# Asking the gate and up weights one section earlier: their two DMAs moved ahead of keys, rows of maxima and value rows in the sync engine's queue

## The chip, the core and the metric

The kernel runs on one core of one Trainium2 chip. The metric is the time of one execution on the device in microseconds (us). A core has five engines that run their own instruction streams: PE (TensorE, matrix products; PEld is its load of stationary data), DVE (VectorE), ACT (ScalarE), POOL (GpSimd) and SP (SyncE), which here issues all DMAs of the main part, one after the other in the order of its queue: an entry that must wait holds up all that stand behind it.

## The reference

```python
x = A_x                                   # 1 x 2048 x 576, float32
xn = _layernorm(x)
s = attention(xn, A_wqkv, A_wo)           # 32 heads of 18 columns, softmax over 2048 keys
g = silu((gelu(xn @ w_gate) * (xn @ w_up)) @ w_down)     # 576 -> 4608 -> 576
return x + s * g
```

## The kernel before

Every float32 operand of a product is cut into a high and a low part (`hi` and `lo`), and three of the four products of parts are summed. The cutting of weights is POOL's work: `split_gu` (lines 156 to 163, its two instructions at lines 131 and 133) cuts one third of a section's gate and up weights into a tile `wh` and a tile `wl`.

**Sections.** The feed-forward part is worked off in 144 sections. The tokens come in 4 blocks of 512; for each block there are 18 rounds of 2 sections, and a section makes 128 of the 4608 hidden columns for 512 tokens: 54 matmuls into `pg` and `pu` (line 548, gate in the upper and up in the lower 64 rows of the array, in pairs that run side by side). Attention is interleaved with it. Sections 0 to 9 are the lead: their extra work is the maxima of the first scores (`pm`, line 1024, reduced by DVE at line 1027). Sections 10 to 137 carry attention: 8 slots each, with scores (`pe`, line 1077, then the exponential on ACT) and the maxima of a later unit. After each odd section come the products with the values (`acc`, line 1112); so an even and an odd section make a pair that repeats. Down products (`py`) follow after a round: in rounds of the lead half of them after each section, in the rounds called PREP (sections 10 to 45, most of the first block and the start of the second) 96 half-height matmuls after each even section (line 616), from section 46 on a seven-product scheme (line 686) that reads prepared weight differences from memory. In PREP POOL also makes those differences for the later rounds: `cut_differences` (lines 730 to 745), queued in each even section behind two of the three weight cuts, reads the raw down weights in the tile `TY`, and its results leave by four stores (`ds`, lines 740 to 743).

**Weights of a section.** `section` for section n asks for the raw weights of section n+1 (`load_gu`, line 148: two DMAs at line 154, gate and up, 288 KB each, into one of two buffers `raw`), and cuts them by thirds while section n's matmuls run. A `wh` has four buffers and a `wl` three, so a third of the next section's `wl` can be written only when the matmuls of section n with the third that stood there are through. `finish` then cuts the section's hidden values (`ah`, `al`) and, after an odd section, the down weights (`bh`, `bl` from `TY`).

**What sets the order.** PE's order is as written. On SP, the loads and stores of sections 2 to 45 are tied by `in_queue` into the order in which the program writes them; the row maxima, value sums, loads of `q` and a few more are placed among them by the scheduler. On POOL, `on_pool` ties the cuts of PREP alone; in the lead and for the multiplication `num` (line 911, numerators of a finished head group by reciprocals `rb`) the scheduler decides where they stand. After a section the program asks, in this order, for rows of maxima (`q<-mT`, line 1066), keys (`Ks` and `Km`, line 962; each ring holds 3 halves and a section uses 2), the gathering of keys in memory (`kx`, lines 981 and 982, only until section 33), new `q`, numerators, sums and value rows (`VS`, line 999). Only then comes the next section, whose first entries are the raw weights for the section behind it, then, in odd sections, the four `ds` stores and the load of `TY` (line 794).

Of the kernel before, what the change touches and what calls it, by code (L numbers as in the profile page):

```python
# [40 lines left out]
G = 2  # L41
NR = F // (G * P)
# [3 lines left out]
PREP = range(ATT.start // G, ATT.start // G + NR)  # L46
# [34 lines left out]
def kernel(ctx: ExitStack, tc: tile.TileContext, x, wqkv, wo, w_gate, w_up, w_down, out):  # L81
# [37 lines left out]
    def chain(name):  # L119

        def keep(i):
            if name in chains:
                no_sync(i, chains[name], "in the order as written")
            chains[name] = i
            return i
        return keep

    in_queue, on_pool = chain("queue"), chain("pool")
# [18 lines left out]
    def raw_wide(n=G * D):  # L147
        return wts.tile([P, G * D], F32, name="raw", bufs=2)[:, 0:n]

    def load_gu(t, keep=lambda i: i):  # L150

        raw = raw_wide().rearrange("p (k n) -> p k n", k=NC)
        for a, w in enumerate((w_gate, w_up)):
            keep(nc.sync.dma_start(raw[HR * a:HR * a + HR], w[:, t * P:(t + 1) * P].rearrange("(k p) n -> p k n", p=HR)))
        return raw, [], []
# [28 lines left out]
    with tc.tile_pool(name="pro", bufs=1) as pro, tc.tile_pool(name="pps", bufs=1, space=PSUM) as pps:  # L184
# [221 lines left out]
        keep = tc.keep_in_program_order  # L406
# [64 lines left out]
        for b in range(NB):  # L471
            for n, t in enumerate(ORDER):
# [6 lines left out]
                if b == 0 and n == len(ORDER) - 1:  # L479
                    nxt = transposes(1, xr)  # L480
# [8 lines left out]
            if b:  # L489
                nxt = transposes(b + 1, xr) if b + 1 < NB else None  # L490
# [4 lines left out]
            if b == 2:  # L495
                ahead = load_gu(0, tc.keep_in_program_order)
# [12 lines left out]
    FF = {"w": ahead, "xd": XD, "down": [], "n": 0, "keep": None, "late": [], "marks": False, "between": [], "added": None,  # L509
          "after": [], "later": [], "soon": [], "stores": []}  # L510
# [8 lines left out]
    def down_pair(t):  # L519
        return t.rearrange("p s n -> p (s n)")[:, 0:G * D].rearrange("p (g n) -> p g n", g=G)  # L520
# [4 lines left out]
    def seven(n):  # L525
        return n // G in SEVEN

    keep = tc.keep_in_program_order
# [268 lines left out]
    def section(specials=(), tag="f", raw_d=None, ahead=True):  # L797

        n = FF["n"]
        FF["n"] += 1  # L800
        b, r = divmod(n // G, NR)
        g = n % G
        pairs, pg, pu = gate_up(tag)
        if g == 0:
            FF["hs"] = []
        pin = tc.keep_in_program_order if seven(n) else kept
        sp_pin = in_queue if 1 < n < PREP.stop * G else kept
        pool_pin = tc.keep_in_program_order if seven(n) else on_pool if n // G in PREP else kept
        keep = sp_pin
        if asked:  # L810
            xd_last = asked.pop()

            def keep(i):
                no_sync(sp_pin(i), xd_last, "transposed x first")
        nxt = None
        if n + 1 < NF:
            nxt = load_gu((n + 1) % (NR * G), keep) if ahead else FF.pop("next_gu")
        if g == G - 1 and FF["stores"]:
            FF["stores"].pop()(sp_pin)
        if g == G - 1 and not seven(n):  # L820
            FF["rawd"] = FF.pop("first_d") if n < G else load_down(
                r, raw_d() if raw_d else down_pair(TY) if n // G in PREP else raw_wide().rearrange("p (g n) -> p g n", g=G), sp_pin) \
                if ahead else FF.pop("next_d")

        def splits(k):
            if nxt and ahead:
                first = split_gu(nxt, k, pool_pin)
                if k == 0 and n in ATT and n > ATT.start and pool_pin is kept:
                    no_sync(first, FF["hl"], "hidden values first")
            x_part(k)  # L830
            if k == 1 and g == 0 and FF["later"]:
                FF["later"].pop()()

        new_x = n + 1 < NF and (n + 1) % (NR * G) == 0
        xd = [[], []]
        if g == G - 1:
            while FF["soon"]:
                FF["soon"].pop(0)()

        def x_part(k):  # L840
            if new_x:
                load_xd_part(b + 1, xd, XG * k, tc.keep_in_program_order if seven(n) else on_pool, sp_pin)

        for k in range(NG - 1):
            pairs[NT_GU * (k + 1)] = lambda k=k, p=pairs[NT_GU * (k + 1)]: (splits(k), p())
        for p in spread(pairs, specials):
            p()
        if nxt and ahead:
            split_gu(nxt, NG - 1, pool_pin)
        FF["w"] = nxt  # L850
        if new_x:
            x_part(NG - 1)
            FF["xd"] = xd
        if g == G - 1 and seven(n):
            load_seven(r)
        FF["act"], FF["rest"] = activate(pg, pu, n < ATT.stop, pin, seven(n) and g == 0)
        now = FF["down"] and FF["down"][0][-1] < FF["n"]
        if n < ATT.stop and not now:
            run_rest()
        if g == G - 1:  # L860
            while FF["after"]:
                FF["after"].pop(0)()

    def run_rest():
        while FF["rest"]:
# [53 lines left out]
    def tasks(n, part):  # L919
        for t in todo.pop((n, part), []):  # L920
            t()
# [21 lines left out]
    with tc.tile_pool(name="att", bufs=1, reuse_waits="tile") as att:  # L943
# [141 lines left out]
        def slot_pairs(s):  # L1085

            u, i = divmod(s, NS)
            um, im = divmod(s + LEAD, NS)

            def pair(h):  # L1090
                for a in range(2):
                    if a == h:
                        score_mm(u, i, a)
                    elif um < NU:
                        max_mm(um, im, a)

            def alone():
                for a in range(2):
                    score_mm(u, i, a, "sm"[a])

            return [lambda h=h: pair(h) for h in range(2)] if um < NU else [alone]
# [57 lines left out]
        for n, m in enumerate(FIRST):  # L1159
            while kept_k < 2 * NA and kept_k * VC < slot + m:  # L1160
                store_k(kept_k, in_queue)
                kept_k += 1
            none = [lambda: None]
            lead = [lambda s=s: lead_pair(s, s == slot + m - 1) for s in range(slot, slot + m)]
            section((m > 0) * (1 + (n == 2)) * none + lead, "s" if n == 1 else "f", lead_raw)
            if slot + m >= NS > slot:
                FF["between"] = max_neg(0, True)
            slot += m
            while n > 1 and chunk < LEAD_K + KB and (chunk - KB + 1) * VC <= slot:
                load_k(chunk, KM, in_queue)  # L1170
                chunk += 1
            if NA <= n < 2 * NA:
                gather_k(n, in_queue)
            if n >= len(FIRST) - KB:
                load_k(n - len(FIRST) + KB, KS, in_queue)
            if n == 3:
                load_q(1)
            if n >= len(FIRST) - 2:
                load_v(n - len(FIRST) + 2)
            full = len(FF["between"]) > 0  # L1180
            downs()
            run_rest()
            finish(cut=split_ap if n < len(FIRST) - 1 else split)
            if full:
                max_rows(0)
        for n in range(NU * NA):
            u, i = divmod(n, NA)
            s0 = n * SLOTS
            sp_pin = in_queue if FF["n"] // G in PREP else lambda i: i
            section([p for s in range(s0, s0 + SLOTS) for p in slot_pairs(s)])  # L1190
            tasks(n, "rows")
            for h in range(2 * n + KB, 2 * n + KB + 2):
                load_k(h, KS, sp_pin)
                load_k(h + LEAD_K, KM, sp_pin)
            gather_k(n + 2 * NA, sp_pin)
            if n == NU * NA - LEAD_K // 2:
                load_wo(flat[0], [(0, 0, k) for k in range(NK)])
            if i == 1 and u + 2 < NU:
                load_q(u + 2)
            tasks(n, 0)  # L1200
            FF["marks"] = u == NU - 1
            um, im = divmod(s0 + LEAD + SLOTS, NS)
            if im == 0 and um <= NU:
                steps = max_neg(um - 1, False)
                cut_at = 2 if FF["down"] and FF["n"] % (NR * G) < NR * G - 8 and FF["down"][0][1] < NR - 1 else 4
                for step in steps[:cut_at]:
                    step()
                FF["between"] = steps[cut_at:]
                at(n + 1, "rows", max_rows, um - 1, sp_pin)
            if i % 2:  # L1210
                for kt in range((i - 1) * VC, (i + 1) * VC):
                    values(u, kt)
                load_v(n + 1, sp_pin)
                load_v(n + 2, sp_pin)
            downs()
            tasks(n, 2)
            finish()
# [187 lines left out]
```

## Time and profile before

| what | value |
|---|---|
| time, median of 3 runs (lowest, highest) | 2673.47 us (2668.4, 2673.79) |
| the profiled execution: its time, its span | 2677.94 us, 2676.2 us |
| mean granted TensorE clock in it | 0.978 |
| busy share: PE, DVE, POOL, ACT | 96%, 77%, 64%, 59% |
| DMA: bytes, mean rate | 528.13 MB, 197 GB/s |

Times in rows are microseconds from the span's start. In the table of stretches an engine's busy time stands with its number of instructions, then the granted clock of TensorE (1.00 is full speed), the busy share of the 16 DMA engines and the rate. In the waits the columns are the total, how many times, the longest. A chain row says when a piece of the chain of work that ended last began, how long it took, and what it was.

### The profile page before, as it was taken

Reading aid. Unit: us, or ns where it says so; the run is one execution under the profiler, and the core shown is the slowest. Engines: PE = TensorE matmul, PEld = TensorE weight load, DVE = VectorE, ACT = ScalarE, POOL = GpSimd, SP = SyncE. Lnnn points to the kernel's source line nnn. Section 1 sums busy time; section 2 is a strip of 40 time slices with the busy share of each in tenths; the row PEclk is TensorE's granted clock in tenths of the full one; section 3 lists DMA queues with packets and bytes.
Section 4 is the critical chain, followed back from the end, with each engine's and each line's share of the span. In section 5 each row is a group of like instructions: output and inputs, shape, how many; then the busy total and the mean of one; then the engine's idle time right before and its main releaser. Section 6 shows DMA issues by size and latency. Waiting matters only on the chain.

```text
span 2676.2 us, 59226 instructions
## 1 busy us (share of the span) xinstructions
PE 2581.8 (96%) x21766; PEld 1954.0 (73%) x21766; DVE 2063.3 (77%) x3621; ACT 1577.0 (59%) x3009; POOL 1721.4 (64%) x2067
## 2 busy tenths in 40 slices
PE   9999898898898998999999999999999999999999
PEld 8888776766665766777776777777776777777688
DVE  5317776776775867899988899999988999998277
ACT  3223365555554655677776667776666676666722
POOL 3135556657557766666667876666667866666785
PEclk9999898999998999999999999999999999999999
DMA  7876466666667667766667777666767777776484
GB/s 251 278 246 158 129 187 202 206 204 210 198 206 213 196 189 214 195 188 189 194 188 201 208 201 195 188 189 193 193 193 204 206 202 191 190 191 182 141 242 142
DMA packets 451381, 528.13 MB, mean 197 GB/s; under 512 B 114826, under 2 KB 312234, under 8 KB 450980
## 3 DMA queue, kind: packets, MB, share of 16 engines
q1 hardware_dynamic: 451092, 524.35, 68.7%
q8 instruction: 173, 2.83, 0.5%
q14 instruction: 116, 0.95, 0.1%
HBM read 424.93 MB, written 113.97 MB: 201 GB/s over the span
## 4 chain that ended last, share of the span: by engine, by line
PE 81%; POOL 8%; DMA 5%; DVE 2%; issue 1%; SPq 1%; ACT 1%; POOLq 0%; ACTq 0%; DVEq 0%
PE pg L548 27%; PE acc L1112 15%; PE py L686 10%; PE pm L1024 8%; PE pe L1077 7%; PE po L210 6%; PE pu L548 3%; PE py L616 3%; PE po L1265 2%; DMA raw<-in_B_w_up_dram 2%; POOL wl L133 2%; POOL TY L734 2%; POOL TY L133 2%; POOL wh L131 1%; DVE mx L1027 1%
## 5 line engine op out<-in xcount | busy, mean ns | idle before, releaser
L1078 ACT ACTIVATE pT<-pe 128x512 f32<-128x512 f32 x2048 | 1154.8, 599 | 535.3 <-PE pm L1024 316.3
L1027 DVE TENSOR_REDUCE mx<-pm 128x1 f32<-128x512 f32 x2048 | 1267.9, 683 | 251.1 <-PE pm L1024 160.1
L548 PE MATMUL pg<-xd,wh 64*128 64x512 f32 x2592 | 958.2, 402 | 53.9 <-POOL wh L131 53.5
L548 PE MATMUL pu<-xd,wh 64*128 64x512 f32 x2592 | 959.2, 403 | 8.4 <-POOL xd L171 7.7
L1077 PE MATMUL pe<-q,Ks 64*128 64x512 f32 x2048 | 795.5, 396 | 7.2 <-DMA Ks<-kx 7.0
L1024 PE MATMUL pm<-Km,q 64*128 64x512 f32 x2048 | 800.2, 398 | 0.8 <-DVE accs L1117 0.5
L548 PEld LDWEIGHTS pg<-xd,wh 64*128 64x128 f32 x2592 | 491.8, 190 | 204.5 <-POOL wh L131 64.4
L133 POOL TENSOR_TENSOR wl<-raw,wh 128x384 fp32r<-128x384 f32 x432 | 441.3, 1022 | 170.9 <-PE pu L548 147.4
L548 PE MATMUL pg<-xd,wl 64*128 64x512 f32 x1296 | 518.7, 400 | 15.3 <-POOL wl L133 15.3
L548 PE MATMUL pu<-xd,wl 64*128 64x512 f32 x1296 | 518.8, 400 | 0.0
L548 PEld LDWEIGHTS pu<-xd,wh 64*128 64x128 f32 x2592 | 492.1, 190 | 15.2 <-POOL xd L171 10.4
L1112 PE MATMUL acc<-pT,VS 128*32 128x512 f32 x4096 | 453.0, 594 | 0.0
L1024 PEld LDWEIGHTS pm<-Km,q 64*128 64x128 f32 x2048 | 384.8, 190 | 44.9 <-DVE mx L1027 7.0
L1077 PEld LDWEIGHTS pe<-q,Ks 64*128 64x128 f32 x2048 | 380.1, 189 | 40.6 <-issue 7.8
L131 POOL TENSOR_SCALAR wh<-raw 128x384 fp32r<-128x384 f32 x432 | 230.1, 533 | 216.0 <-DMA raw<-in_B_w_up_dram 132.5
L1112 PEld LDWEIGHTS acc<-pT,VS 128*32 128x32 f32 x4096 | 127.0, 110 | 291.4 <-issue 279.5
L548 PEld LDWEIGHTS pg<-xd,wl 64*128 64x128 f32 x1296 | 246.6, 190 | 70.0 <-POOL wl L133 27.3
L133 POOL TENSOR_TENSOR al<-t,ah 128x512 fp32r<-128x512 f32 x264 | 265.0, 1004 | 22.0
L548 PEld LDWEIGHTS pu<-xd,wl 64*128 64x128 f32 x1296 | 246.3, 190 | 2.4
L686 PE MATMUL py<-bh,ah 128*128 128x288 f32 x630 | 191.3, 304 | 0.5 <-DVE Y L695 0.5
L686 PE MATMUL py<-bl,ah 128*128 128x288 f32 x630 | 186.5, 296 | 0.0
L686 PE MATMUL py<-bh,al 128*128 128x288 f32 x630 | 185.9, 295 | 0.0
(199 smaller groups left out, 3784.3 us busy)
## 6 DMA issues: line engine op xcount, KB each, us to landing
Ks<-kx SPq DMA_DIRECT2D x256, 256.0 KB
Km<-kx SPq DMA_DIRECT2D x248, 256.0 KB
bh<-ds SPq DMA_DIRECT2D x45, 1008.0 KB
bl<-ds SPq DMA_DIRECT2D x45, 1008.0 KB
raw<-in_B_w_gate_dram SPq DMA_DIRECT2D x144, 288.0 KB
raw<-in_B_w_up_dram SPq DMA_DIRECT2D x144, 288.0 KB
VS<-vs SPq DMA_DIRECT2D x128, 152.0 KB
qk<-t SPq DMA_DIRECT2D x72, 256.0 KB
```

The source lines that it names most:

```text
L131: first = nc.gpsimd.tensor_scalar(hi, raw, 1.0, 1.0, op0=ALU.mult, op1=ALU.mult)
L133: low_part[:] = [keep(nc.gpsimd.tensor_tensor(lo, raw, f(hi), op=ALU.subtract))]
L210: nc.tensor.matmul(o, st, m, start=(i == 0), stop=(i == len(TERMS) - 1))
L548: nc.tensor.matmul(o, w[1 + wp][k][rr, c, :], xd[xp][k][rr, c, :], start=(i == 0), stop=(i == len(terms) - 1))
L616: return nc.tensor.matmul(py, hs[g][a][rr, j * P:(j + 1) * P], wd[w][rr, g, 288 * c:288 * c + 288], start=start, stop=stop)
L686: nc.tensor.matmul(py, x[:, a, t * P:(t + 1) * P], y[:, w, :], start=(i == 0), stop=(i == 2))
L734: on_pool(nc.gpsimd.tensor_tensor(raw[:, to], raw[:, x], raw[:, y], op=ALU.subtract))
L1024: nc.tensor.matmul(pm, QS[u, r][rr, t * P:(t + 1) * P], keys(KM, u, c, r)[rr, :], start=True, stop=True)
L1027: return nc.vector.tensor_reduce(MX[u][:, 2 * r + a, t, c:c + 1], pm, axis=AX.X, op=ALU.max)
L1077: nc.tensor.matmul(pe, keys(KS, u, c, r)[rr, t * P:(t + 1) * P], QS[u, r][rr, :], start=True, stop=True)
L1078: nc.scalar.activation(PT[u, kt][:, 2 * r + a, :], pe, AF.Exp, scale=SCALE)
L1112: nc.tensor.matmul(ACC[u][32 * a:32 * a + 32, :], VS[(u * NA + c) % VB][:, v:v + 32], pt[:, a, :], start=first, stop=last, skip_group_chec ...
```

## The change

A function `ask_weights` is called right behind each section of the lead and of attention. For sections 3 to 46 it asks for the raw weights of the section after the next one there and then, tied into the queue's order; the next call of `section` takes what was asked instead of asking itself. So the request for the weights of section n+2 moves from the head of section n+1 to the tail of section n, in front of the rows of maxima, the keys, the gathers, the numerators and the value rows that follow section n. Buffers, cuts and matmuls stay.

```diff
         if n + 1 < NF:
-            nxt = load_gu((n + 1) % (NR * G), keep) if ahead else FF.pop("next_gu")
+            nxt = FF.pop("next_gu", None) or load_gu((n + 1) % (NR * G), keep)
...
+    def ask_weights():
+
+        n = FF["n"] + 1
+        if 2 < n <= PREP.stop * G:
+            FF["next_gu"] = load_gu(n % (NR * G), in_queue)
...
             section((m > 0) * (1 + (n == 2)) * none + lead, "s" if n == 1 else "f", lead_raw)
+            ask_weights()
...
             section([p for s in range(s0, s0 + SLOTS) for p in slot_pairs(s)])
+            ask_weights()
             tasks(n, "rows")
```

The orders of PE, DVE and ACT stay the same but for one exchange of two neighbours on ACT in the lead. Line numbers behind the new function are 6 to 8 higher.

**SP, an odd section of PREP and what follows it.** Before (`q_4179` and `q_4188` are the query tiles that get rows of maxima, `ds_145` a round's differences):

```order
L154 DMA raw<-in_B_w_gate_dram 64x9x128
L154 DMA raw<-in_B_w_up_dram 64x9x128
L740 DMA ds_145<-TY 128x1152
L741 DMA ds_145<-bh 128x2016
L742 DMA ds_145<-bl 128x288
L743 DMA ds_145<-bl 128x1152
L794 DMA TY<-in_B_w_down_dram 128x2x576
L1066 DMA q_4179<-mT_75 1x16x32 x4
L1066 DMA q_4188<-mT_75 1x16x32 x4
L962 DMA Ks<-kx_113 128x512
L962 DMA Km<-kx_118 128x512
```

The same place now:

```order
L740 DMA ds_145<-TY 128x1152
L741 DMA ds_145<-bh 128x2016
L742 DMA ds_145<-bl 128x288
L743 DMA ds_145<-bl 128x1152
L794 DMA TY<-in_B_w_down_dram 128x2x576
L154 DMA raw<-in_B_w_gate_dram 64x9x128
L154 DMA raw<-in_B_w_up_dram 64x9x128
L1072 DMA q_4182<-mT_75 1x16x32 x4
L1072 DMA q_4191<-mT_75 1x16x32 x4
L968 DMA Ks<-kx_113 128x512
L968 DMA Km<-kx_118 128x512
```

The two `raw` rows here are not the same request: before, they are cut in this very section; now the requests for this section stand nine rows ahead of the first one shown, and those shown are for the section after it. They stand behind the differences' stores and in front of rows of maxima and keys.

**POOL, the lead.** `al` is the low part of a section's hidden values (`t_2743` is section 4, `t_2927` section 5); `wh` and `wl` between them are thirds of the weights of the section that comes next. Before:

```order
L133 TENSOR_TENSOR wl<-raw,wh 128x384
L141 TENSOR_TENSOR al<-t_2743,ah 128x512
L141 TENSOR_TENSOR al<-t_2927,ah 128x512
L131 TENSOR_SCALAR wh<-raw 128x384 x2
L133 TENSOR_TENSOR wl<-raw,wh 128x384 x2
```

Now:

```order
L131 TENSOR_SCALAR wh<-raw 128x384
L141 TENSOR_TENSOR al<-t_2743,ah 128x512
L133 TENSOR_TENSOR wl<-raw,wh 128x384
L131 TENSOR_SCALAR wh<-raw 128x384
L133 TENSOR_TENSOR wl<-raw,wh 128x384
L131 TENSOR_SCALAR wh<-raw 128x384
L133 TENSOR_TENSOR wl<-raw,wh 128x384
L141 TENSOR_TENSOR al<-t_2927,ah 128x512
```

Before, the cuts for section 6 stand behind section 5's hidden values, and the same holds for sections 7, 8 and 9. Now the cuts for sections 6, 7 and 9 stand in front of the hidden values; those for sections 8 and 10 stand behind them, the latter as a new place.

**POOL, a pair of PREP.** The multiplication `num` for the first half of a group, before, right behind the down weights of an odd section:

```order
L131 TENSOR_SCALAR bh<-TY 128x1152
L133 TENSOR_TENSOR bl<-TY,bh 128x1152
L911 TENSOR_TENSOR num<-num,rb 72x256
L131 TENSOR_SCALAR wh<-raw 128x384
L133 TENSOR_TENSOR wl<-raw,wh 128x384
```

Now, behind the hidden values of the even section that follows:

```order
L131 TENSOR_SCALAR ah<-t_6191 128x512
L133 TENSOR_TENSOR al<-t_6191,ah 128x512
L917 TENSOR_TENSOR num<-num,rb 72x256
L131 TENSOR_SCALAR wh<-raw 128x384
L133 TENSOR_TENSOR wl<-raw,wh 128x384
```

So two thirds of the weight cuts and the differences of that section now stand in front of `num`, and the second half's `num` moves in the same way from the even section to the odd one.

## Prediction

> **What bounds the kernel now.** I read the table of stretches first, to see where PE stands still, then the waits of the worst stretch, then the chain of work through it, then the queues of POOL and SP at those times.
>
> Stretches of the profile before (the first two are the lead and PREP, then four single pairs of PREP, then the four sections after it):
>
> ```profile
> core 0: us, PE busy (x) PEld busy (x) DVE busy (x) ACT busy (x) POOL busy (x), PEclk, DMA share, GB/s
> 191.00:339.50 148.50, 134.42 (x1233) 118.09 (x1234) 102.18 (x178) 55.97 (x124) 79.00 (x84) 0.91 0.57 148
> 339.50:1014.30 674.80, 614.31 (x5697) 452.34 (x5700) 479.60 (x839) 388.24 (x762) 428.20 (x467) 0.94 0.67 202
> 867.20:902.30 35.10, 33.88 (x336) 25.50 (x340) 27.56 (x48) 22.36 (x45) 23.37 (x25) 1.00 0.64 197
> 902.30:936.50 34.20, 33.62 (x336) 25.34 (x337) 28.46 (x52) 22.95 (x46) 24.21 (x27) 1.00 0.74 198
> 936.50:980.10 43.60, 37.32 (x338) 26.00 (x340) 28.36 (x49) 22.61 (x45) 27.34 (x32) 0.92 0.70 194
> 980.10:1014.30 34.20, 33.57 (x338) 25.54 (x340) 28.72 (x51) 22.73 (x46) 24.32 (x26) 1.00 0.66 212
> 1014.30:1093.20 78.90, 71.00 (x615) 53.72 (x615) 58.50 (x100) 45.90 (x88) 49.78 (x62) 0.94 0.70 197
> 1093.20:2550.00 1456.80, 1450.27 (x12233) 1048.78 (x12234) 1264.14 (x2213) 1004.86 (x1874) 1029.85 (x1302) 1.00 0.70 192
> ```
>
> From 1093 us on PE is busy for 1450 of 1457 us at full clock; the change does not reach there. In PREP 60.5 us of 674.8 are idle and the clock is 0.94. PREP holds 17 pairs (value products of section 11 at 339.52 to those of section 45 at 1014.32), 39.7 us each; yet three of the four late pairs, which have no gathers of keys in SP's queue, take 35.1, 34.2 and 34.2 us with the same matmuls and the same POOL work.
>
> Value products in the chain, which mark the ends of pairs:
>
> ```profile
> 339.52 7.00 PE acc L1112 x64
> ...
> 1014.32 7.00 PE acc L1112 x64
> ...
> 1093.24 7.00 PE acc L1112 x64
> ...
> 1454.32 7.00 PE acc L1112 x64
> ...
> 1525.26 7.00 PE acc L1112 x64
> ```
>
> Waits within PREP:
>
> ```profile
> POOL wh L131 <- DMA raw<-in_B_w_up_dram: 74.5, 10, 14.9
> PE pg L548 <- POOL wh L131: 42.3, 16, 3.3
> POOL num L911 <- DMA rb<-rT: 37.6, 6, 7.7
> PE pg L548 <- POOL wl L133: 10.1, 23, 1.1
> PE pe L1077 <- DMA Ks<-kx: 1.7, 1, 1.7
> PEld acc L1112 <- DMA q<-mT: 0.9, 3, 0.3
> ```
>
> PE's idle time is 42.3 + 10.1 = 52.4 us of waiting for cut weights, and POOL in turn stood waiting for raw weights or, in front of them in its queue, for reciprocals. Keys and rows of maxima are hardly ever late. The chain through one pair shows the loop:
>
> ```profile
> 533.35 6.88 DMA TY<-in_B_w_down_dram
> ...
> 545.80 7.14 DMA rb<-rT
> 553.07 0.75 POOL num L911
> 554.00 5.49 DMA raw<-in_B_w_up_dram
> ...
> 562.84 0.78 POOL TY L734
> ...
> 570.52 0.49 POOL wh L131
> 571.08 1.00 POOL wl L133
> 572.13 0.79 PE pg L548
> ```
>
> Read it so: SP issues `TY`, keys and gathers, then `rb`, and only at 554.0 the raw up weights, which land at 559.5; POOL cuts two thirds, makes the differences (562.84 to 570.52, 7.7 us), cuts the last third, and PE, which has waited for it, goes on at 572.1. The differences' end frees SP's next stores, and the loop starts again. It takes the pair's 40 us; PE's own work would take 34.
>
> **The change, term by term.**
>
> *PREP.* The request for a section's weights moves from after to before the keys, gathers, numerators and value rows, about a section earlier, while the weights are needed no earlier. In the chain they land at 559.5 within the section that cuts them; with at least half a section (about 8 us) gained they wait for POOL, and the loop through SP is cut: the cuts then follow PE's own progress. What is late next? An even section's matmuls take from 505.66 to 515.55, 9.9 us:
>
> ```profile
> 505.66 0.50 PE L548 MATMUL pg<-xd,wh 64*128 64x512 f32 x1
> ...
> 515.55 0.32 PE L616 MATMUL py<-bh,ah 64*128 64x288 f32 x2
> ```
>
> Two thirds are through 6.6 us in, a `wl` later (1.0) the differences start and end at 6.6 + 1.0 + 7.7 = 15.3 us after the section's start; the last third is cut by 17, and PE needs it two thirds into the odd section, about 16.5 + 6.6 = 23. So POOL keeps 6 us in hand, as its busy time of 24 in a pair of 34 says too. The next bound is PE itself, as in the undisturbed pairs: (35.1 + 34.2 + 34.2)/3 = 34.5 us. 17 x 34.5 = 586.5. The change of token block lies in PREP once; in the later pairs, 32.8 us each ((1454.32 - 1093.24)/11), two pairs with it take 70.9 instead of 65.6, so 5.3 more: 591.8 against 674.8, **a gain of 83.0 us**. Between ends: 17 x 34.2 without the extra gives 93, and half the gain is rival 1.
>
> Part of this is the clock, since idle time alone is 60.5 us. In the lead the same is seen at one stop:
>
> ```profile
> 249.81 0.79 PE L548 MATMUL pg<-xd,wh 64*128 64x512 f32 x1 [2.85 <-POOL wh L131]
> ```
>
> ```profile
> 252.04 0.42 PE pg L548
> ...
> 256.19 0.23 PE pg L548
> ```
>
> After 2.85 us of idleness the steps take 0.42 us until 256, then 0.23. [...]
>
> *Lead.* Cuts for sections 6 to 9 stand in POOL's queue behind the hidden values of the section before, which wait for ACT; PE waits at each:
>
> ```profile
> 265.07 1.26 POOL L141 TENSOR_TENSOR al<-t,ah 128x512 fp32r<-128x512 f32 x1 [8.76 <-ACT ah L140]
> ```
>
> ```profile
> PE pg L548 <- POOL wh L131: 11.2, 4, 2.9
> PE pg L548 <- POOL wl L133: 2.6, 4, 0.6
> ```
>
> That is (11.2 + 2.6)/4 = 3.45 us a stop, and some 10 steps at 0.42 instead of 0.23, 1.9 us: 5.35 us. The order now has such a place at sections 8 and 10 alone, so two stops of four go: **10.7 us**. Between ends: nothing (if the raw weights still come late) and 4 x 5.35 = 21.
>
> *What is moved past.* Each request is two issues and 576 KB. On SP an issue took
>
> ```profile
> 554.00 0.63 SPq L154 DMA_DIRECT2D raw<-in_B_w_up_dram  x1
> ```
>
> so two take 1.3 us, and 576 KB at the 202 GB/s of PREP are 2.9 us: up to 4.2 us later, by estimate, for whatever stands behind. In an odd section these are the rows of maxima and the keys, which were asked at
>
> ```profile
> 534.61 6.23 SPq L1066 DMA_DIRECT2D q<-mT  x8
> 540.94 0.38 SPq L962 DMA_DIRECT2D Ks<-kx  x1
> ```
>
> while the value products ahead of the next section ended at 536.56 + 7.07 = 543.6:
>
> ```profile
> 536.56 7.07 PE L1112 MATMUL acc<-pT,VS 128*32 128x512 f32 x64
> ```
>
> The rows were out 2.8 us before they were used, the keys 7.7 us before the second half of the section, 5 us in, reads them. That would be too tight for 4.2 us more, if the place stayed. But this stretch of SP's queue begins when POOL ends the differences, and that end moves against PE: before, 13 us ahead of the next even section (570.5 less 40 is 530.5, against 543.6), now 34.5 - 15.3 = 19 us. So the stretch begins 6 us earlier and is 4.2 us longer. The cover is 2 us thick; if it is gone, each section pays up to 4.2. I take 0.3 us a pair, **5 us in all**, with nothing and 34 x 4.2 = 143 as the ends; the reason to stay near the lower one are the 1.7 and 0.9 us of waits for keys and rows.
>
> POOL's `num` moves behind two thirds of the cuts and the differences. It no longer holds up the cuts (37.6 us of waiting for `rb`), which is within the gain above; but SP's store of its result stands ahead of the next load of `rb`, and three of the four stores of differences wait behind that. This delays `TY` and the keys in every second pair by some 8 us by estimate (19.6 instead of 15.3 us for `num`, and a store's way to memory), which the 6 us that POOL has in hand nearly hide.
>
> *Sections 46 to 49* (1014.3 to 1093.2) lose 78.9 - 2 x 32.8 = 13 us to the change of down scheme; the order of SP changes there in details only. I take 0, with -6 and +6 as ends.
>
> **The sum.** -83.0 - 10.7 + 5 + 0 = -88.7. The profiled execution took 2677.94 us, which gives 2589.2; it lies 4.5 above the median of 2673.47, so I forecast **2585 us**. If the stops gave back their idle time alone, it would be 60.5 less 17 x 0.8 that the good pairs keep, and 6.9 in the lead, less the 5: 48.6 us, 2625. With the ends of the terms (93, 21, 0, -6) the best case is 2673.5 - 120 = 2553.
>
> **The rivals.** A measurement of this kernel can tell a change from none at about 0.2%, 5 us.
>
> 1. *Half the gain: another wait in every second pair.* The chain num, store, `rb`, three stores, `TY`, down weights holds POOL in the pairs that hold both `num`. For it: SP waits for POOL and memory at several of these entries already. Against: by the times above PE has 6 us to spare. Time: -41.5 - 10.7 + 5 = -47, 2626. Chance 0.20.
>
> 2. *Slower: keys become just in time.* If the stretch of SP's queue does not begin earlier, each section's keys land up to 4.2 us later, and the 2 us of cover are gone: 34 x 4.2 = 143 us lost against 93.7 gained, +49, 2723. It decides from the point where PE waits for `Ks` by over 2.8 us a section. For it: weights, differences and `TY` (2.9 MB together) stand in front of the keys. [...] Against: 1.7 us of waits for keys before. Chance 0.04.
>
> 3. *The idle time goes, the clock stays low* by other short stops: 2625, as worked out in the sum. For it: the clock in the lead was 0.91. Against: the good pairs have 1.00, and the steps after the stop at 249.8 show that stops of this length do cost clock. Chance 0.06. [...]
>
> 4. *No change.* The request is earlier in the program but not in time, since in odd sections it stands behind the stores that wait for POOL's differences, and POOL remains the pace. Against: such weights are needed only a section later, and POOL is busy for 24 of 34 us. Time 2673, chance 0.05.
>
> **How the numbers follow.** The forecast has 0.65, its own range from 2555 to 2605. Rivals 1 and 3 lie at 2626 and 2625; a range from 2560 to 2640 holds most of the forecast (0.60) and most of these (0.23), together 0.83. Faster by over 0.2%: 0.65 + 0.20 + 0.06 = 0.91; within: 0.05; slower: 0.04.
>
> **What would show it.** Right: in PREP pairs of 34 to 35 us between value products, clock near 1.00, POOL's wait for raw weights gone from 74.5 to under 15 us, two stops of PE in the lead instead of four, keys later in SP's queue but PE waiting for them by under 10 us. Wrong: pairs that alternate between 34 and over 37 (rival 1, with POOL waiting for `TY` or `rb`), PE waiting for `Ks` or `q` in most sections (rival 2), clock under 0.97 with the waits gone (rival 3), or POOL still waiting for raw weights (rival 4). A gain under 35 us would mean that the loop through SP was not what held the pairs.

## The result, and the profile after

The kernel after takes **2653.27 us** (median of 4 runs, 2648.81 to 2656.5), before 2673.13 (4 runs, 2668.4 to 2673.79): ratio 0.9928, 95% interval 0.9909 to 0.9947. It is faster, by 20 us and not by the 88 of the forecast. The profiled execution took 2648.81 us with a span of 2647.0, against a span of 2676.2 before; its clock is 0.986 (0.978). The two profiled executions lie 29 us apart and the medians 20, because the one before is 4.8 us above its median and the one after 4.5 below its own; the gains by stage below add up to the 29 and are so 9 us too large together.

Stretches of the kernel after, with the columns as in the prediction: the lead; PREP; then two parts of PREP, its first twelve pairs (those with gathers) and its last four (without); sections 46 to 49; the rest that was compared before.

```profile
191.00:330.43 139.43, 128.12 (x1234) 114.53 (x1236) 102.32 (x178) 56.10 (x124) 82.46 (x90) 0.96 0.62 160
330.43:981.00 650.57, 598.59 (x5696) 469.63 (x5700) 490.91 (x839) 387.83 (x762) 431.06 (x462) 0.96 0.73 208
330.36:795.39 465.03, 424.90 (x4035) 333.55 (x4033) 348.71 (x592) 273.81 (x540) 296.25 (x319) 0.96 0.70 205
844.43:980.93 136.50, 132.70 (x1320) 105.67 (x1312) 112.58 (x195) 89.65 (x177) 99.03 (x107) 1.00 0.77 214
981.00:1060.08 79.08, 70.03 (x615) 51.48 (x618) 56.23 (x100) 45.78 (x88) 49.61 (x62) 0.96 0.70 204
1060.08:2520.00 1459.92, 1452.81 (x12240) 1051.72 (x12242) 1265.80 (x2214) 1004.78 (x1874) 1030.40 (x1304) 1.00 0.71 192
```

The same two parts of PREP in the kernel before:

```profile
339.45:817.52 478.07, 434.93 (x4034) 321.55 (x4033) 337.27 (x592) 274.33 (x539) 294.31 (x324) 0.94 0.65 201
867.13:1014.25 147.12, 138.41 (x1331) 102.41 (x1329) 113.12 (x196) 90.67 (x179) 99.31 (x108) 0.98 0.69 200
```

The lead ends 9.1 us earlier (339.5 to 330.4). PREP takes 650.6 us instead of 674.8, 24.2 less. Of these 10.6 come from the four pairs without gathers, which are now 34.1 us each at full clock, as forecast. The twelve pairs with gathers give only 13.0: they went from 39.8 to 38.75 us. PE's idle time in PREP fell from 60.5 to 52.0 us and no further. Sections 46 to 49 are the same (79.1, before 78.9).

Waits of PE in PREP after (total, times, longest), where in the kernel before 42.3 and 10.1 us stood for cut weights:

```profile
PE pe L1083 <- DMA q<-mT: 27.0, 6, 5.7
PE py L616 <- DVE Y L604: 9.6, 13, 1.2
PE pe L1083 <- DMA Ks<-kx: 8.1, 5, 4.4
```

No wait of PE for `wh` or `wl` is left in PREP, nor POOL's 74.5 us for raw up weights. The change did what it says. In their place stand rows of maxima (27.0) and keys (8.1), which the request was moved past: the waits changed hands, 54 us before (42.3 + 10.1 + 1.7) and 45 in these three rows. The wait for `Y`, DVE's adding up of down products, is new too.

Lead of the kernel after, PE's waits:

```profile
PE pg L548 <- POOL wh L131: 5.8, 2, 2.9
PE py L616 <- POOL bl L141: 2.3, 1, 2.3
PE py L616 <- ACT bh L140: 1.6, 1, 1.6
PE pg L548 <- POOL wl L133: 1.6, 2, 0.9
```

Two stops of four are gone, as the order said. The two rows in the middle are a new stop: PE's down products wait 3.9 us for cut down weights. So PE's idle time in the lead falls only from 14.1 to 11.3 us, and 6.3 of the 9.1 us come from its busy time, at a clock of 0.96 instead of 0.91.

The chain through one pair of PREP after, which answers to the chain before that ended in the cut of `wh`:

```profile
548.55 0.74 POOL num L917
549.31 5.10 DMA oN<-num
554.47 0.67 SPq L907
...
557.40 1.11 SPq L794
558.56 1.25 SPq L154
559.86 1.13 SPq L154
561.03 0.62 SPq L968
561.70 9.38 DMA Km<-kx
...
599.80 0.67 SPq L1072
600.51 6.61 DMA q<-mT
```

It runs through the DMA queue now: a store of 72 KB takes 5.1 us, a load of keys of 256 KB 9.4 us, and one of the eight requests for rows of maxima, 2 KB each, 6.6 us. In the whole of the chain between 330 and 1093 us `Km` has 5.2%, `q<-mT` 4.6% and `Ks` 3.1%.

### The profile page after: what moved, and what is told of

Its sections match the earlier page's. It is cut to its first block, busy times and chain, and to the rows that moved or that the text cites. A ratio compares the mean times of both kernels' runs of the same rounds, so it can differ in the third digit from the quotient of the medians.

```text
span 2647.0 us, 59224 instructions
## 1 busy us (share of the span) xinstructions
PE 2560.3 (97%) x21766; PEld 1967.1 (74%) x21766; DVE 2076.7 (78%) x3621; ACT 1576.1 (60%) x3009; POOL 1728.1 (65%) x2067
## 4 chain that ended last, share of the span: by engine, by line
PE 81%; DMA 7%; DVE 4%; POOL 3%; issue 1%; SPq 1%; ACT 1%; POOLq 0%; ACTq 0%; DVEq 0%
PE pg L548 26%; PE acc L1118 13%; PE py L686 9%; PE pm L1030 8%; PE pe L1083 8%; PE po L210 7%; PE pu L548 4%; PE py L616 4%; PE po L1273 2%; DMA Km<-kx 2%; DVE mx L1033 2%; DMA q<-mT 1%; DVE t L588 1%; DMA Ks<-kx 1%; POOL wl L133 1%
## 5 line engine op out<-in xcount | busy, mean ns | idle before, releaser
L548 PE MATMUL pg<-xd,wh 64*128 64x512 f32 x2592 | 943.2, 396 | 8.4 <-POOL wh L131 5.8
L548 PE MATMUL pu<-xd,wh 64*128 64x512 f32 x2592 | 942.5, 396 | 6.6 <-POOL xd L171 6.6
L1083 PE MATMUL pe<-q,Ks 64*128 64x512 f32 x2048 | 787.3, 394 | 36.6 <-DMA q<-mT 27.0
L1030 PE MATMUL pm<-Km,q 64*128 64x512 f32 x2048 | 791.2, 395 | 2.8 <-DMA Km<-kx 1.5
L548 PEld LDWEIGHTS pg<-xd,wh 64*128 64x128 f32 x2592 | 483.4, 187 | 139.4 <-POOL ah L131 30.2
L548 PE MATMUL pg<-xd,wl 64*128 64x512 f32 x1296 | 508.8, 393 | 3.5 <-POOL wl L133 3.4
L548 PE MATMUL pu<-xd,wl 64*128 64x512 f32 x1296 | 508.6, 392 | 0.0
L548 PEld LDWEIGHTS pu<-xd,wh 64*128 64x128 f32 x2592 | 483.7, 187 | 12.4 <-POOL xd L171 8.7
```

The source lines that it names most:

```text
L548: nc.tensor.matmul(o, w[1 + wp][k][rr, c, :], xd[xp][k][rr, c, :], start=(i == 0), stop=(i == len(terms) - 1))
L1030: nc.tensor.matmul(pm, QS[u, r][rr, t * P:(t + 1) * P], keys(KM, u, c, r)[rr, :], start=True, stop=True)
L1083: nc.tensor.matmul(pe, keys(KS, u, c, r)[rr, t * P:(t + 1) * P], QS[u, r][rr, :], start=True, stop=True)
```

## The experiments

Four theories were set against each other. A: SP's queue is the pace by the number and order of its entries, since it issues its DMAs one after the other (0.46 us an issue, the median of the 736 in PREP of the kernel after). B: the weights in front alone make rows and keys late. C: the mean rate of the memory is used up by PREP's 17 MB in two pairs (214 GB/s in the kernel after). D: one kind of transfer, the gathers of keys, keeps most of the 16 DMA engines idle (their busy share rests at 0.3 or 0.2 for stretches of the kernel after, rows at run 10) and holds up what stands behind it. All runs of one group were made on one chip, beside the kernel before.

**1. Rows of maxima back in front of the weights.**

```diff
             section([p for s in range(s0, s0 + SLOTS) for p in slot_pairs(s)])
-            ask_weights()
             tasks(n, "rows")
+            ask_weights()
```

> The changed kernel, but in the attention sections the weights are asked behind the rows of maxima instead of in front of them. Theory A (serial queue: from the store of the first numerators to the rows of maxima SP's queue is one chain that sets two pairs; every microsecond taken from it comes off): the rows lose 1.3 us of issues and up to 2.9 us of transfer in front of them, so 1.3 to 4.3 us less for every two pairs with gathers, 6 times: 8 to 26 us faster than the changed kernel, and PE's 27 us of waiting for rows in PREP falls to 5 to 20. Theory B (only the weights in front make the rows late): the waits of 27 us vanish with the slow clock behind them, 35 to 45 us faster. Theory C (the memory rate, not the order, sets these pairs): no difference, within 5 us.

Measured: 2638.55 us (2634.47 to 2638.82), ratio 0.9861 (0.9848 to 0.9875), 15 us faster than after. PE's waits in PREP of this run:

```profile
PE pe L1083 <- DMA Ks<-kx: 14.7, 6, 4.0
...
PE pe L1083 <- DMA q<-mT: 4.8, 4, 1.8
```

The wait for rows went from 27.0 to 4.8 us, but the one for keys from 8.1 to 14.7, and PREP still takes 641.0 us. The 15 us lie where A has them (8 to 26) and under the 35 to 45 of B: the weights' place in front of the rows costs some 15 us, which is more than the forecast's 5 and far less than PREP lacks.

**2. The second half of a group's numerators a section later**, to take apart the chain `num`, store, reciprocals, stores, `TY` of the prediction's first rival.

```diff
-                    at((u + 1) * NA + 3 + h, 2 * h, load_piece, u, h)
-                    at((u + 1) * NA + 4 + h, 2 * h, norm_piece, u, h)
+                    at((u + 1) * NA + 3 + 2 * h, 0, load_piece, u, h)
+                    at((u + 1) * NA + 4 + 2 * h, 2 * h, norm_piece, u, h)
```

> The changed kernel, but numerators and reciprocals of the second half of a head group are loaded one section later, behind the keys of the odd section, and multiplied one section later, so that the stores of weight differences no longer stand behind a load that waits for the first half's store to land (2.0 to 4.0 us at each such place). Theory A: 2 to 5 us less for every two pairs with gathers, 10 to 30 us faster than the changed kernel. Theory B: no difference, since the weights stay in front of the rows. Theory C: no difference, within 5 us.

Measured: 2656.43 us (2653.39 to 2658.17), ratio 0.9929 (0.9917 to 0.9942), the same as after. PE waits for rows by 33.4 us. Thinning out that chain brings nothing here: the pairs alternate between 35 and 43 us.

**3 and 4. The gathers off SP's queue**, issued by ACT behind the section's square, in the kernel after and in the kernel before.

```diff
-                    keep(nc.sync.dma_start(kx[m][:, n * DH:(n + 1) * DH, :], qk[i, rows, cols].rearrange("(h d) s -> h d s", d=DH)))
+                    no_sync(nc.scalar.dma_start(kx[m][:, n * DH:(n + 1) * DH, :], qk[i, rows, cols].rearrange("(h d) s -> h d s", d=DH)),
+                            FF["square"], "the section's square first")
```

(and the ones below it in the same way)

> The changed kernel, but the gathering of keys in memory (4 DMAs a section) is issued by ACT, behind the section's square, instead of SP. The bytes are the same; SP's queue loses about 12 to 13 us of issuing for every two pairs, ACT gains as much. Theory A: pairs fall from 39.6 to 34.5 to 36 us, 40 to 60 us faster than the changed kernel, and the waits for rows of maxima go. Theory B: the rows are still behind the weights but SP is earlier altogether, so it makes no separate statement. Theory C: the same bytes in the same time, no difference within 10 us.

> The kernel before, without the change, with the gathers issued by ACT. Theory A (SP's queue is the pace of the pairs with gathers before the change too): about 6 us less in each of 12 pairs until PE's 34.5 us bound them, 40 to 60 us faster than before. Theory B (before the change, the late weights alone were the bound): the weights are asked about 2.5 us earlier in each section, 20 to 40 us faster. Theory C: no difference.

Measured: 2882.65 us (ratio 1.0778, 1.0763 to 1.0793) and 2827.8 us (1.0572, 1.0557 to 1.0586). Both are far slower. ACT's own sequence in the first of them (start, length, in brackets the idle time in front and what ended it):

```profile
525.33 8.44 ACTq L987 DMA_DIRECT2D kx<-qk  x2
533.80 0.59 ACTq L989 DMA_DIRECT2D kx<-ones  x1
534.44 2.07 ACT L1085 ACTIVATE pT<-pe 128x512 f32<-128x512 f32 x4 [19.12 <-DMA kx<-qk]
```

The row of 8.44 us joins two issues, of 0.59 and 0.57 us, with 7.3 us between them; the 69 issues of such gathers by ACT between 330 and 970 us take 0.57 to 0.60 us each. For the rest ACT waits for transfers of SP: in this run's trace ACT and SP share eight semaphores that tell of landings, and the second issue waits for the one that SP's load of `sums`, issued at 527.0, raised last at 533.17; the first had waited for value rows in the same way, 10.0 us. Behind these waits stand ACT's exponentials, idle for 19.1 us. So these two runs price waits of ACT for SP's transfers, and they don't decide between A, C and D.

**5 and 6. The gathers with rows outermost**, in the kernel after and in the kernel before. The same bytes in the same pieces of 512 elements are named in another order: 18 rows by 4 heads instead of 4 heads by 18 rows, and the ones as 10 by 4 by 512 instead of 4 by 5120.

```diff
-                    keep(nc.sync.dma_start(kx[m][:, n * DH:(n + 1) * DH, :], qk[i, rows, cols].rearrange("(h d) s -> h d s", d=DH)))
-                keep(nc.sync.dma_start(kx[m][:, MROW:HR, :], ones.rearrange("(o r) t -> o r t", o=1)
-                                       .to_broadcast([QD, HR - MROW, TB])))
+                    keep(nc.sync.dma_start(kx[m][:, n * DH:(n + 1) * DH, :].rearrange("h d s -> d h s"),
+                                            qk[i, rows, cols].rearrange("(h d) s -> d h s", d=DH)))
+                keep(nc.sync.dma_start(kx[m][:, MROW:HR, :].rearrange("h r t -> r h t"), ones.rearrange("r (o t) -> r o t", o=1)
+                                       .to_broadcast([HR - MROW, QD, TB])))
```

> The changed kernel, but the gathering DMAs have the 18 (or 10) rows as their outermost dimension instead of the 4 heads; same bytes, same number of DMAs, same 2 KB runs. Theory D (new: the gathers keep only about 5 of 16 DMA engines busy, seen as stretches of 0.3 in the DMA share, and all that stands behind them in the ring waits for those engines; that is the pace of the pairs with gathers): the stretches of 0.3 go, pairs fall from 39.6 to 34.5 to 36.5 us, 35 to 60 us faster than the changed kernel, 2593 to 2618, with under 10 us of waiting for rows and keys. Theory A (the number and order of SP's entries is the pace): the entries are the same, so within 8 us of the changed kernel.

> The kernel before, without the change, with the gathers' rows outermost. Theory D: the loop of 39.7 us through SP and POOL has one gather in each section, 4 to 5 us of engine time of which half goes: 3 to 5 us less in each of 12 pairs, 35 to 60 us faster than before. The first reading (before the change the late weights alone held the pairs): the weights still stand behind keys and gathers and land 2 us earlier a section at most, 10 to 25 us faster.

Measured: 2584.53 us (2581.26 to 2589.06; ratio 0.9661, 0.9647 to 0.9676) and 2632.37 us (2631.65 to 2640.55; 0.9848, 0.9833 to 0.9864). Stretches of the kernel after with these gathers (lead, twelve pairs, the pair with the change of token block, four pairs):

```profile
191.00:313.08 122.08, 122.08 (x1230) 112.51 (x1228) 101.48 (x178) 55.97 (x124) 83.09 (x90) 1.00 0.71 182
313.08:736.26 423.18, 408.58 (x4034) 322.89 (x4032) 345.54 (x592) 273.24 (x539) 296.44 (x319) 1.00 0.78 226
736.26:781.03 44.77, 37.51 (x333) 28.34 (x333) 28.46 (x52) 23.06 (x46) 35.00 (x36) 0.92 0.89 222
781.03:920.48 139.45, 134.23 (x1331) 104.21 (x1329) 113.01 (x197) 90.83 (x179) 100.56 (x108) 1.00 0.77 216
```

and of the kernel before with them (lead, twelve pairs):

```profile
191.00:318.41 127.41, 123.50 (x1232) 111.73 (x1230) 102.17 (x178) 55.95 (x124) 81.14 (x87) 1.00 0.66 175
318.41:768.16 449.75, 426.19 (x4035) 325.95 (x4033) 335.35 (x592) 274.30 (x539) 294.86 (x321) 0.96 0.68 213
```

Run 5 gains more over the kernel after (69 us) than the 35 to 60 expected, though rows and keys still wait for 12.2 us (8.0 + 4.2) and not under 10; run 6 gains 43, as D has it. The twelve pairs take 35.3 us each after, 37.5 before. PREP takes 607.4 and 647.8 us (values from 313.08 to 920.48 and from 318.41 to 966.17). C falls, since the same bytes go at 226 instead of 205 GB/s, and A falls too: it had run 5 within 8 us of the kernel after, for the entries on SP are the same. Waits in PREP of the kernel before with spread gathers:

```profile
POOL wh L131 <- DMA raw<-in_B_w_up_dram: 111.9, 14, 11.6
PE pg L548 <- POOL wh L131: 24.8, 14, 3.3
```

The late weights, which the change removes, are still late there. With the gathers spread the change is worth 2632.4 - 2584.5 = 48 us; with the gathers as they were, 20. On POOL and, for a few rows, on SP the scheduler answered this edit with some exchanges, so it is repeated below with less.

**7. Both: rows in front and spread gathers.** (The edits of 1 and 5.)

> The changed kernel with both: weights behind the rows of maxima, and the gathers' rows outermost. Theory D: once the gathers are spread the rows are no longer late, so the place of the weights adds little: within 8 us of the variant with spread gathers alone. Theory A: what the place of the weights gave (14.7 us) is all that is to be had: 2635 to 2642.

Measured: 2583.96 us (2581.24 to 2587.3), ratio 0.9661 (0.9648 to 0.9674), no different from run 5. Once the gathers are spread, the rows' place in the queue costs nothing in the whole time; by the profiles the twelve pairs take 416.3 us, 34.7 each, instead of 423.2.

**8 and 9. The earlier request in the lead alone, and in PREP alone.**

```diff
-        if 2 < n <= PREP.stop * G:
+        if 2 < n <= len(FIRST):
```

```diff
-        if 2 < n <= PREP.stop * G:
+        if len(FIRST) < n <= PREP.stop * G:
```

> The change in the lead alone (weights of sections 3 to 10 asked ahead, all later ones as before). The prediction's term for the lead: 10.7 us faster than before, with two stops of PE instead of four; the first value products then come 9 to 12 us earlier (330.4 to 331 instead of 339.5), and nothing changes behind them but that the pairs of PREP follow at 39.7 us.

> The kernel after with the earlier request only from the first section behind the lead on (the lead as before). If the terms add, as the run with the lead alone (9 us of gain) suggests: the gain of PREP alone, 11 us, so 2662 us, 2657 to 2667. If the lead's earlier requests are what puts PREP's queue in order: near 2674.

Measured: lead alone 2666.04 us (2665.09 to 2672.71) beside 2675.21, ratio 0.997 (0.996 to 0.9979); PREP alone 2654.69 us (2647.84 to 2660.75) beside 2674.6, ratio 0.9924 (0.9907 to 0.9941). In the first, PE's largest wait in PREP is as before:

```profile
PE pg L548 <- POOL wh L131: 43.1, 18, 3.3
```

So 9 us belong to the lead when it is changed by itself, by the medians. In the profile of that run the first value products come at 333.0, 6.5 us earlier than before and not the 9 to 12 expected. PREP alone gave 20 and not the 11 expected: it can't be told from the whole change. By the profiles the two add up (PREP alone: values at 339.6 and 993.3, so 653.7 us of PREP, and a span of 2659.0 against 2647.0), but that profile is of its slowest run. Whether the lead's 9 us come on top stays open.

**10. Only the gathers of keys turned**, the ones left at 4 by 5120.

> The kernel after with only the gathers of keys turned (rows outermost, 18x4x512); the gathers of ones stay with 4 heads outermost (4x5120). Theory D (a gather whose outermost dimension has 4 entries keeps about 5 of 16 DMA engines busy and holds up what stands behind it): the keys are 288 rows of 512 elements for each block's tile, the ones 40 a tile in long pieces, so most of the gain of 69 us comes with the keys: 2590 to 2615 us. If the ones were as bad as the keys: 2620 to 2640. Theory C (the mean rate of memory sets the pairs): no change from 2653.

Measured: 2589.3 us (2585.3 to 2593.93), ratio 0.9685 (0.9667 to 0.9703). It lies just under the 2590 to 2615 of D. This is the cleanest test: the order on PE, DVE and SP is that of the kernel after, and POOL's and ACT's differ in the lead alone. Its lead, twelve pairs and block change:

```profile
191.00:313.16 122.16, 122.16 (x1232) 112.38 (x1230) 101.48 (x178) 55.96 (x124) 82.29 (x90) 1.00 0.73 183
313.16:741.85 428.69, 412.19 (x4035) 326.45 (x4033) 346.01 (x592) 273.54 (x540) 297.05 (x319) 0.99 0.76 222
741.85:789.63 47.78, 40.39 (x333) 29.64 (x332) 28.85 (x52) 23.00 (x46) 35.13 (x36) 0.86 0.92 231
```

PE's waits in its PREP:

```profile
PE py L616 <- DVE Y L604: 9.9, 13, 1.4
PE pe L1084 <- DMA q<-mT: 7.9, 4, 2.6
PE pe L1084 <- DMA Ks<-kx: 2.8, 1, 2.8
```

The twelve pairs fall from 465.0 to 428.7 us, PREP from 650.6 to 613.7 (to the values at 926.83), with nothing but the outer dimension of the gathers changed there. The lead ends 17.2 us earlier; since POOL's order differs there, that part is not put down to the transfers alone. Rows wait 7.9 instead of 27.0. The busy share of the DMA engines over the same two pairs, in 40 slices, and the rate, in the kernel after (556.6 to 637.2 us, slices of 2.0 us):

```profile
DMA  9999998333235799689939991296333789933849
GB/s 388 344 302 195 183 190 267 123 116 134 68 102 122 200 221 309 247 343 392 401 156 254 247 149 45 40 319 199 115 121 112 169 213 230 374 130 126 325 163 410
```

and in this one (522.7 to 594.4, slices of 1.8 us):

```profile
DMA  9999998532346899799999981388534899964789
```

Leaving out the two slices with 0.1 and with 0.2 or 0.3 in the middle, where the queue is nearly empty, the share stands at 0.3 or 0.2 for 11 slices after, 22 us of 80.6; here for 4, 7 us of 71.7. The first such stretch, five slices behind the key loads, moves 68 to 134 GB/s. (Twelve loads of new `q`, 36 KB each, stand behind the gathers there, and in run 10 that place still moves 73 to 133 GB/s over four slices.) A share of 0.3 is that of 5 of 16 engines. Each of the 69 gathers of keys in PREP raises its semaphore 5 times after, once 1.05 us behind the start of its issue (median) and four times when it lands, and 10 times here; a load of keys does so 16 times. So 5 raises go with a share of 0.3 and the 16 of the key loads with one of 0.9 or 0.8; that the gathers kept about 5 engines busy is an estimate from these numbers. The three gathers of a tile land 1.41 us behind one another after (median; 105 GB/s for 144 KB) and 0.63 us here (234 GB/s).

Why does that hold up others? The 736 DMAs of PREP in the kernel after, each an entry of SP's queue, take eight semaphores in turn, and none of them goes out before the DMA eight entries ahead of it has raised its semaphore for the last time. So a gather that lands late stops SP itself, at a load of `q` or a store, and late stores stop it at the load of `TY`. SP's longest waits show it. After:

```profile
SPq L794 <- DMA ds<-TY: 21.5, 8, 3.7
SPq L1020 <- DMA kx<-qk: 19.3, 18, 1.1
SPq L914 <- DMA kx<-qk: 15.2, 15, 1.2
```

In run 10:

```profile
SPq L794 <- DMA ds<-TY: 7.2, 7, 1.8
SPq L1021 <- DMA kx<-qk: 5.8, 16, 0.7
```

All waits of SP for gathers of keys and ones together take 51.5 us in PREP after and 13.1 in run 10.

**11. Spread gathers and the later second half.** (The edits of 5 and 2.)

> The kernel after with spread gathers (2584.5 us) and with the second half of each group's numerators moved one section later as in the second run. If, with the DMA queue relieved, the chain numerators, store, reciprocals, differences' stores and down weights (the forecast's first rival) still costs the pairs of 36 to 37 us: 2570 to 2580. If not: 2581 to 2588, no change.

Measured: 2597.1 us (2595.44 to 2603.02), ratio 0.9718 (0.97 to 0.9735), outside both expectations: 13 us slower than run 5. Its first twelve pairs are better (416.6 against 423.2 us), but the five after them take 195.1 instead of 184.2, and what follows is 12 us longer (its profile is of its slowest run, 6 us above the median). What makes the late pairs longer was not traced. Run 5 or 7 stays the best.

## Why the prediction was wrong

**The step that failed** is in the PREP term: "The next bound is PE itself, as in the undisturbed pairs". It carried 34.5 us, read from pairs without gathers, to the twelve pairs that have them. These take 465.0 us and not 12 x 34.5 = 414, and these 51 us are most of the 59 by which PREP (650.6) is above the 591.8 of the term; the pair with the change of token block has 9 more. What holds the twelve pairs is the queue behind the gathers: for stretches it moves at 68 to 134 GB/s, at a busy share of the DMA engines of 0.3 or 0.2. With that failed "What is moved past", put at 5 us: it priced rows and keys by the two issues (1.3 us) and by 576 KB at PREP's mean rate of 202 GB/s (2.9 us), and called 2 us of cover enough. In the kernel after the cover was gone in 11 places: 27.0 + 8.1 us of waiting, with the clock that goes with it (0.96).

The runs take the 51 us of the twelve pairs apart. Turning the gathers of keys alone (run 10) takes off 36.3, rows back in front alone (run 1) 13.1, and both together, with the ones turned too (run 7), 48.7. So the gathers are the larger part, and the weights' place in front of the rows the smaller, but more than the 5 us that the forecast gave to all that was moved past. I had seen that the undisturbed pairs were those "which have no gathers of keys in SP's queue" and read it as entries on SP; it was the transfers.

**The PREP term** (17 pairs to 34.5) had the right end and the wrong condition. Pairs without gathers took 34.1, and with spread gathers the kernel after has 35.3 over the first twelve, 34.7 with the rows in front as well (run 7). The pair of 39.7 us had two limits of nearly the same length: the loop through late weights (37.5 us when the gathers are spread, run 6) and the queue behind the gathers (38.75 when the weights are early). The change removed the first alone. That run 5 comes out at the 2585 us forecast is partly chance: 43 us of it (2675.2 less 2632.4) are the gathers' own gain, 48 the change's, of which the lead has 5.3 and PREP 40.4.

**The change of token block** was put at 5.3 us over a pair of 34.5. It is 49.0 us after, 14.5 more, and 10.3 more even in run 5.

**The lead** came out near in size, -10.7 forecast and -9.1 measured, with two stops of four gone; in part that is luck, since a new stop of 3.9 us took back idle time and the clock gave more than forecast. Changed by itself (run 8) it gave 9.2 us by the medians and 6.5 by the profile.

**Sections 46 to 49** were right at nothing (+0.2). Behind them the kernel after takes 3.9 us longer to the span's end (1586.9 against 1583.0), which no step foresaw and no run explains.

**The clock**: that stops of under 3.3 us cost clock holds in the traces of this case, though not for every such stop (2.3 us at 953.9 in the kernel before left it at 1.00). Behind the stop of 2.85 us in the lead before, which the forecast shows, the granted clock is 0.50 from 249.1 to 255.9 us and 1.00 in the 10.2 us that follow; behind one of 2.9 us in the lead after it is 0.50 from 272.1 to 275.5 us. Run 10 shows it too: its pair with the block change has single waits of at most 2.8 us, three of them close together, and a clock of 0.86. In the whole of PREP the idle time fell by 8.5 us and the busy time by 15.7 for the same matmuls, the clock rising from 0.94 to 0.96 and not to 1.00, and 52.0 us of stops remained.

**The rivals.** The first (numerators hold POOL in every second pair) named the right picture, pairs that alternate between 37 and 42 us, and the wrong cause: run 2 moved that chain and gained nothing. Only with the gathers spread does moving it shorten the twelve pairs, by 6.6 us (run 11). The second had the right mechanism, rows and keys just in time, in fewer places: 11 waits in PREP and not 34; so it took back a part of the gain and did not turn the sign. (The weights, differences and `TY` that it counts in front of the keys are 3.5 MB together and not 2.9.) The keys that it speaks of (256 KB) took 9.4 us to land in the kernel after, behind stores, down weights and raw weights. The third (low clock with the waits gone) does not hold, since the waits were not gone (its sum comes to 48.8 us, not 48.6); nor does the fourth, since POOL no longer waits for raw up weights. The line "a gain under 35 us would mean that the loop through SP was not what held the pairs" was too strict: the loop held them, and something else held them nearly as long.

## What to carry to other kernels

Before a request is moved forward in a queue, read how fast that queue moves at that place, from the DMA share in slices of a microsecond or two, and not from a stage's mean rate: here the share rested at 0.3 or 0.2 behind the gathers, at 68 to 134 GB/s against the 205 of the twelve pairs, and turning the gathers took 36.9 us off PREP. Then look in the waits of the issuing engine for entries that stand until that transfer has landed. When undisturbed stretches lack two things at once (late weights, gathers), remove each by itself before the whole difference is booked to one. Naming the same bytes with the longer dimension outermost brought the kernel after three times what the reordering had brought (69 against 20 us), and the kernel before twice as much (43 against 20 us).

## What the runs showed of the hardware

- A gather of 4 by 18 by 512 elements (144 KB) in place of 18 by 4 by 512 cost this kernel 64 us (2653.3 against 2589.3) at 28 tiles of 3 gathers each, though in the lead the scheduler's order on POOL changed too; in PREP, where nothing else changed, it cost 36.9. Turning the 4 by 5120 of ones as well gave 5 us more, which the intervals of the two runs do not tell from nothing.
- Such a gather raised its semaphore 5 times with the heads outermost and 10 times with the rows outermost, and landed 1.41 and 0.63 us behind the one in front of it.
- Gathers issued by ACT took 0.57 to 0.60 us each to issue, but ACT, and its exponentials with it, stood for landings of SP's transfers on the semaphores that both share: 17.3 of the 19.1 us shown. These kernels took 7.8% and 5.7% longer than the kernel before.
